# Attention and max-out feed-forward on one core: early columns first, casts shared, w's first half for both token spans, some loads later

## The chip, the core and the metric

One core of a Trainium2 chip runs the whole program. The metric is device time in microseconds (us); a run's *span*, from the first to the last instruction in the trace, is about 1.8 us shorter than its time. The kernel before takes 282.14 us (median of 3 runs, 282.08 to 282.3). Beside the experiments it ran again on four chips, from 282.14 to 286.01 in all, so every experiment is compared with runs of the kernel before from its own rounds, on the same chip. In the views PE is TensorE (it multiplies matrices), DVE is VectorE, ACT is ScalarE (here the exps and some copies), POOL is GpSimd and SP is SyncE (here it issues loads). PSUM is the memory that TensorE writes, SBUF the one that it reads.

## The reference, cut to what matters

```python
# q, k, v: (8 batches, 8 heads, 576 tokens, 64), float32
scores = q @ k.T / 8, masked so that 64-token block i sees blocks j <= i
x = (softmax(scores) @ v)               # -> (4608 tokens, 512)
g = maximum(x @ w1, x @ w2)             # (4608, 1024)
out = g @ w_out                         # (4608, 512)
```

## The kernel before: the parts that matter here

Heads are handled in pairs, two pairs to a group; a batch has 4 pairs (groups 0 and 1). A group's q and k are loaded, cast to bf16 (16-bit floats), transposed on TensorE, and copied from PSUM to SBUF. Scores of a pair come in bursts (p: the first 256 query tokens; q1, q2, q3: the rest), each followed by one exp on ACT. `av` multiplies by v and normalises, `x_out` transposes the result into x. Feed-forward matmuls (h: 8 *steps* for one 128-column slice f of w1 and w2) are poured in between by `fill`, in the order of a list of units; a unit waits until its tokens of x exist.

```python
def cast(nm, g, parts):                       # parts: (engine's copy, first, last row group)
    ...
def load_qk(g, queues, gated=False):          # gated: a small GpSimd memset of the target makes
    ...                                       # the DMA wait until GpSimd gets to this point
# order of issue in the opening
load_qk(1, (SP, SP)); load_qk(2, (SP, None))
...
load_v(0, 0); load_v(0, 1); load_w(0, 256, (0,))
cast("k", 1, ((pool, 0, RPP),))
load_w(0, 256, (1,)); load_qk(2, (None, SP), gated=True)
...
# TensorE order of the opening, cut
warm_up(16)                                   # 16 matmuls of zeros, "fillers"
...
burst_p(0); masks_p(0); burst_p(1); warm_up(2); masks_p(1)
load_v(0, 2); load_v(0, 3); load_v(0, 4); load_w(256, 256)
burst_q1(0); load_w(512, 512); warm_up(3)
burst_p(2); av(0, [0, 1]); burst_q3(0); warm_up(2); burst_p(3); ...
cast("q", 2, ((pool, 0, RPP),)); masks_q(0); cast("k", 2, ((pool, 0, RPP),))
burst_q2(1); x_out(1, 0, 2); ...              # the first h may start after this x_out
for c in range(3): load_v(1, c)
fill(2); load_qk(3, (SP, SP), gated=True)
...
masks_q(3); ...; fill(3)
tile_0(4), tile_1(4); av(3, [2, 3, 4]); fill(5); x_out(1, 2, NCH)   # end of batch 0's attention
# units: for each token span i, all 8 slices f
for i in range(NSPAN):
    for f in range(NFF):
        h(i, f)
```

GpSimd (POOL) is not only a caster: it issues the loads of v and w, writes the masks, and its memsets open the gates of the later q, k loads, all in program order.

The softmax here doesn't subtract the row's maximum and nothing guards it: scores larger than these inputs give would overflow.

Of the kernel before, what the change touches and what calls it, by code (L numbers as in the profile page):

```python
# [9 lines left out]
BF16 = mybir.dt.bfloat16  # L10
# [4 lines left out]
def kernel(  # L15
# [10 lines left out]
    nc = tc.nc  # L26

    B, H, S, D = q.shape
    P = 128
# [6 lines left out]
    NFF = d_ff // P  # L36
# [6 lines left out]
    NP = 64  # L43
    RPP = S // NP
# [9 lines left out]
    NCH = 5  # L54
# [3 lines left out]
    QCUT = 256  # L58
# [14 lines left out]
    NSPAN = len(spans)  # L73
# [37 lines left out]
    def load_qk(g, queues, gated=False):  # L111
        b, u = divmod(g, GPB)
        for nm, src, queue in (("q", q, queues[0]), ("k", k, queues[1])):
            if queue is None:
                continue
            raws[nm, g] = t = raw.tile([P, 2, RPP * D], FP32, name=f"{nm}raw")
            if gated:
                nc.gpsimd.memset(t[:, 0, :1], 0.0)
            queue.dma_start(
                out=t[:],  # L120
                in_=src[b, 4 * u:4 * u + 4].rearrange(
                    "(s h) (p t) d -> (h p) s (t d)", h=2, t=RPP),
            )

    def cast(nm, g, parts):
        t = raws.pop((nm, g)).rearrange("p s (t d) -> p t s d", d=D)
        qk_n[nm, g] = n = qkn.tile([P, RPP, 2, D], BF16, name=f"{nm}n")
        for copy, j0, j1 in parts:
            copy(out=n[:, j0:j1], in_=t[:, j0:j1])  # L129

# [11 lines left out]
    def load_w(f0, fw, which=(0, 1)):  # L142
        for i in which:
            dst, src = ((w1_sb, w1r), (w2_sb, w2r))[i]
            nc.gpsimd.dma_start(out=dst[:, :, f0:f0 + fw], in_=src[:, :, f0:f0 + fw])
# [11 lines left out]
    nc.vector.memset(zeros[:], 0.0)  # L157
    nc.scalar.activation(out=warm[:], in_=warm[:], func=AF.Exp)
    load_qk(1, (SP, SP))
    load_qk(2, (SP, None))  # L160
    make_identity(nc, ident)
    for r in range(NV):
        nc.vector.memset(vv_r[r][:, :, :, D:D + 1], 1.0)
# [7 lines left out]
    for c in range(2):  # L171
        load_v(0, c)
    load_w(0, 256, (0,))
    cast("k", 1, ((pool, 0, RPP),))
    load_w(0, 256, (1,))
    load_qk(2, (None, SP), gated=True)


    done_tokens = [0]
# [64 lines left out]
    def plan():  # L244
        def h(i, f):
            t0, w = spans[i]
            units.append((h_unit(i, f), t0 + w, w / SPAN, 2 * NDM))

        def y(i, s, last=False):
            t0, w = spans[i]  # L250
            if last:
                units.append((y_last(i, s), t0 + w, 0.333, 3 * NFF))
            else:
                units.append((y_unit(i, s), t0 + w, 1.0, NFF))

        for i in range(NSPAN):
            for f in range(NFF):
                h(i, f)
                if i > 2 and f % 2 == 0 and f // 2 < tiles[i - 1]:
                    y(i - 1, f // 2)  # L260
            if i == 1:
                for j in range(2):
                    for s in range(tiles[j]):
                        y(j, s)
        n = tiles[-1]
        for s in range(n):
            y(NSPAN - 1, s, s == n - 1)
# [13 lines left out]
    def fill(n):  # L281
        while n > 0 and at[0] < len(steps) and steps[at[0]][1] <= done_tokens[0]:
            u, _, cost = steps[at[0]]
            next(u)
            n -= cost
            at[0] += 1


    def warm_up(n):
        pw = ps_m.tile([P, SPAN], FP32, name="ps_w", tag="m")  # L290
        for _ in range(n):
            nc.tensor.matmul(pw[:], zeros[:, :P], zeros[:], start=True, stop=True)  # L292
# [4 lines left out]
    def transposes(nm, g, copies):  # L297
        n = qk_n.pop((nm, g))
        pts = [ps_m.tile([P, RPP, NP], BF16, name=f"ps_{nm}T", tag="m") for _ in range(2)]
        for j in range(RPP):  # L300
            for i in range(2):
                r = slice(i * NP, (i + 1) * NP)
                nc.tensor.transpose(  # L303
                    pts[i][:, j, :], n[r, j].rearrange("p s d -> p (s d)"), ident[r, r],
                )

        def copy_out(which=(0, 1)):
            for i in which:
                t = (qT_r if nm == "q" else kT_r)[(2 * g + i) % NT]
                copies[i](  # L310
                    out=t[:, :S].rearrange("q (p j) -> q p j", j=RPP),
                    in_=pts[i].rearrange("q j p -> q p j"),
                )
        return copy_out

# [44 lines left out]
    def burst_p(p):  # L360
        burst(p, ((0, 0, QCUT), (1, P, QCUT - P)), 0)

    def burst_q1(p):
        burst(p, ((0, QCUT, 320), (1, QCUT, 192)), 384)

    def burst_q2(p):
        burst(p, ((1, 448, P), (2, QCUT, 320), (4, 512, BLK)), 896)
# [4 lines left out]
    def masks_p(p, eng=None):  # L372
        for a in (0, 256):
            mask(p, a, eng)

    def masks_q(p, eng=None):
        for a in (1024, 1408):
            mask(p, a, eng)
# [34 lines left out]
    def av(p, ts):  # L413
        b, hp = divmod(p, HP)
        vv = vv_r[b % NV]
        a = aT_r[p % NA]
        n = len(ts)
        h0 = hp // 2 * 4 + hp % 2
        if p % 2 == 0 and ts[0] == 0:
            xps[p // 2] = xpool.tile([P, NCH, 2, 2, D], BF16, name="xp")  # L420
        xp = xps[p // 2]
        po = ps_m.tile([P, n, 2, D + 1], FP32, name="ps_o", tag="m")
        n_mm = 2 * sum(t + 1 for t in ts)
        mm = 0
        for gi, t in enumerate(ts):
            for hh in range(2):
                for c in range(t + 1):
                    a0 = a_col(p, c, t)
                    nc.tensor.matmul(  # L429
                        po[:, gi, hh, :], a[:, hh, a0:a0 + P], vv[:, c, h0 + 2 * hh, :],  # L430
                        start=(mm == 0), stop=(mm == n_mm - 1),
                    )
                    mm += 1
        rec = small.tile([P, 3, 2, 1], FP32, name="rec")
        nc.vector.reciprocal(rec[:, :n, :, 0], po[:, :, :, D])  # L435
        nc.vector.tensor_mul(  # L436
            xp[:, ts[0]:ts[0] + n, :, p % 2], po[:, :, :, :D],
            rec[:, :n].to_broadcast([P, n, 2, D]),
        )

    def x_out(g, t0=0, t1=NCH):
        b, u = divmod(g, GPB)
        xp = xps[g]
        n = t1 - t0
        n_odd = min(t1, NCH - 1) - t0
        pe = ps_m.tile([P, 2, n, BLK], BF16, name="ps_xe", tag="m")
        po = ps_m.tile([P, 2, n_odd, BLK], BF16, name="ps_xo", tag="m")
        for s in range(2):
            for t in range(t0, t1):
                src = xp[:, t, s].rearrange("p a d -> p (a d)")  # L450
                nc.tensor.transpose(pe[:, s, t - t0, :], src[:BLK], ident[:BLK, :BLK])  # L451
                if t < NCH - 1:
                    nc.tensor.transpose(po[:, s, t - t0, :], src[BLK:], ident[BLK:, BLK:])
        dst = xT[:, 2 * u:2 * u + 2, b * S + t0 * P:b * S + t1 * P].rearrange(
            "p s (t h w) -> p s t h w", h=2, w=BLK)
        nc.vector.tensor_copy(out=dst[:, :, :, 0], in_=pe[:])  # L456
        nc.vector.tensor_copy(out=dst[:, :, :n_odd, 1], in_=po[:])
        if u == GPB - 1:
            done_tokens[0] = min(b * S + t1 * P, (b + 1) * S)

# [37 lines left out]
        return lambda: [f() for f in outs]  # L498


    warm_up(16)
    cq = transposes("q", 0, (dve, act))
    ck = transposes("k", 0, (act, dve))
    cq((0,))
    ck((0,))
    cq((1,))
    ck((1,))
    cast("q", 1, ((dve, 0, RPP),))
    burst_p(0)
    masks_p(0)  # L510
    burst_p(1)
    warm_up(2)
    masks_p(1)
    for c in range(2, NCH):
        load_v(0, c)
    load_w(256, 256)
    cq = transposes("q", 1, (dve, dve))
    burst_q1(0)
    ck = transposes("k", 1, (dve, dve))
    for i in range(2):  # L520
        cq((i,))
        ck((i,))
    load_w(512, 512)
    warm_up(3)
    burst_p(2)
    av(0, [0, 1])
    burst_q3(0)
    warm_up(2)
    burst_p(3)
    masks_p(2, nc.vector)  # L530
    av(1, [0, 1])
    masks_p(3, nc.vector)
    burst_q2(0)
    av(2, [0, 1])
    warm_up(2)
    burst_q1(1)
    av(3, [0, 1])
    x_out(0, 0, 2)
    warm_up(2)
    cast("q", 2, ((pool, 0, RPP),))  # L540
    masks_q(0)
    cast("k", 2, ((pool, 0, RPP),))
    burst_q2(1)
    x_out(1, 0, 2)
    warm_up(2)
    burst_q3(1)
    masks_q(1)
    for c in range(3):
        load_v(1, c)
    fill(2)  # L550
    load_qk(3, (SP, SP), gated=True)
    burst_q1(2)
    transposes("q", 2, (dve, act))()
    fill(3)
    burst_q2(2)
    av(0, [2, 3, 4])
# [5 lines left out]
    av(1, [2, 3, 4])  # L562
    fill(2)
    burst_q1(3)
    transposes("k", 2, (dve, act))()
    pad_keys(4)
    pad_keys(5)
    fill(2)
    x_out(0, 2, NCH)
    burst_q2(3)  # L570
    av(2, [2, 3, 4])
    fill(2)
    burst_q3(3)
# [87 lines left out]
```

## Time and profile before

| | before |
|---|---|
| time, span | 282.14 us, 280.4 us |
| TensorE busy, share of the chain that ended last | 96%, 91% |
| mean granted TensorE clock | 1.000 |
| fillers | 29 |
| first h, steps done before the last x_out of batch 0 | 18.09 us, 40 |
| q, k of group 2: cast by GpSimd at | 17.20, 18.81 us |

The prediction below shows the chain and TensorE's opening (start, duration, engine, line, operation, tiles; in brackets the idle time before it and what ended that). Here is the row of events that turned out to decide the case, GpSimd in order of time (start, duration, engine, line, operation, tiles; in brackets the idle time before it and what ended that):

```profile
17.20 1.14 POOL L129 CAST qn<-qraw 128x1152 bf16<-128x1152 f32 x1
...
18.81 1.15 POOL L129 CAST kn<-kraw 128x1152 bf16<-128x1152 f32 x1
...
20.30 2.64 POOL L133 DMA_DIRECT2D vv<-in_v_dram  x3
...
22.99 0.10 POOL L118 MEMSET qraw<- 128x1 f32 x1
...
23.19 0.34 POOL L350 MEMSET aT<- 64x128 bf16 x2
...
26.06 0.20 POOL L350 MEMSET aT<- 64x128 bf16 x1 [0.45 <-ACT aT L345]
...
29.60 1.15 POOL L129 CAST qn<-qraw 128x1152 bf16<-128x1152 f32 x1 [2.44 <-DMA qraw<-in_q_dram]
```

Group 2 is cast early, without waiting for its data. So the next three v issues, the gate of group 3 (22.99) and the masks of pair 2 (23.19) are all on time; those of pair 3 (from 26.06) waited for the exp and not for GpSimd. The 2.44 us of waiting at 29.60 show up in no TensorE wait: nothing urgent stands behind that cast.

### The profile page before, as it was taken

The numbers are of one execution on the slowest core, as the hardware profiler recorded it, in microseconds if no ns is written. First come the engines' busy times: TensorE is split into PE (matmuls) and PEld (weight loads), VectorE is DVE, ScalarE is ACT, GpSimd is POOL, SyncE is SP. The second block draws the span as 40 slices with busy tenths as digits, with TensorE's granted clock in tenths as the row PEclk, the third lists the DMA queues.
The fourth block names the chain that finished last, engine by engine and source line by source line (L and its number), as shares of the span: only waits on it lengthen the run. The fifth ranks groups of instructions, "written<-read, shape, count | busy, mean of one in ns | idle before, by whom it ended". The sixth has DMA issues, their size and how long they took to land.

```text
span 280.4 us, 7767 instructions
## 1 busy us (share of the span) xinstructions
PE 269.3 (96%) x3208; PEld 151.5 (54%) x3253; DVE 185.7 (66%) x386; ACT 139.6 (50%) x194; POOL 107.7 (38%) x271
## 2 busy tenths in 40 slices
PE   7699999999999999999999999999999999999995
PEld 2356766655556455555555554646455644444543
DVE  5967879668887676767667576757655766365430
ACT  3786577667664664655647374664653000100112
POOL 2996446764654625164344625371120000000000
PEclk9999999999999999999999999999999999999999
DMA  7999999979934994479266866175301111111114
GB/s 261 263 219 220 187 244 273 250 148 189 210 42 153 154 156 78 178 82 239 49 208 77 219 75 196 52 81 50 67 5 49 49 54 40 39 75 40 73 41 150
DMA packets 55940, 36.68 MB, mean 131 GB/s; under 512 B 38752, under 2 KB 43232, under 8 KB 55904
## 3 DMA queue, kind: packets, MB, share of 16 engines
q0 software_dynamic: 41728, 7.87, 35.0%
q1 hardware_dynamic: 13760, 27.66, 28.8%
q10 hardware_dynamic: 416, 0.66, 0.7%
q8 instruction: 25, 0.41, 0.6%
q14 instruction: 11, 0.09, 0.1%
HBM read 34.60 MB, written 9.44 MB: 157 GB/s over the span
## 4 chain that ended last, share of the span: by engine, by line
PE 91%; DMA 4%; issue 2%; ACT 1%; DVE 1%; POOL 0%; ACTq 0%
PE ps_h L197 43%; PE ps_y L215 22%; PE ps_o L429 11%; PE ps_s L321 8%; DMA vv<-in_v_dram 2%; PE ps_xe L451 2%; PE ps_qT L303 2%; DMA qraw<-in_q_dram 2%; PE ps_kT L303 2%; ACT aT L345 1%; PE ps_s L339 1%; PE ps_y L231 1%; PE ps_w L292 1%; DVE g L206 0%; POOL vv L133 0%
## 5 line engine op out<-in xcount | busy, mean ns | idle before, releaser
L197 PE MATMUL ps_h<-xT,w_sb 128*128 128x512 bf16 (+3 forms) x605 | 136.2, 357 | 1.7 <-issue 0.3
L345 ACT ACTIVATE aT<-ps_s 128x1024 bf16<-128x1024 f32 (+2 forms) x100 | 96.2, 996 | 17.2 <-PE ps_s L321 16.2
L197 PEld LDWEIGHTS <-w_sb 128*128 128x128 bf16 x640 | 57.8, 98 | 57.4 <-issue 8.1
L204 DVE CAST h<-ps_h 128x512 bf16<-128x512 f32 (+3 forms) x80 | 50.9, 637 | 28.9 <-PE ps_h L197 26.7
L215 PE MATMUL ps_y<-wo_sb,g 128*128 128x512 bf16 x273 | 65.5, 379 | 2.1 <-PE ps_s L321 1.3
L206 DVE TENSOR_TENSOR g<-h,ps_h 128x512 bf16<-128x512 bf16 (+3 forms) x80 | 50.6, 632 | 12.0 <-PE ps_h L197 10.5
L350 POOL MEMSET aT<- 64x128 bf16 x124 | 22.3, 199 | 92.7 <-ACT aT L345 91.3
L221 ACT COPY y<-ps_y 128x512 f32<-128x512 f32 x31 | 18.1, 584 | 70.3 <-PE ps_y L215 56.5
L429 PEld LDWEIGHTS <-aT 128*128 128x128 bf16 x960 | 37.3, 98 | 14.1 <-issue 1.3
L215 PEld LDWEIGHTS <-g 128*128 128x128 bf16 x280 | 26.8, 98 | 30.4 <-issue 1.1
L429 PE MATMUL ps_o<-vv,aT 128*128 128x65 bf16 x960 | 39.9, 194 | 0.3 <-DMA vv<-in_v_dram 0.3
L133 POOL DMA_DIRECT2D vv<-in_v_dram x40 | 33.7, 847 | 0.5
L436 DVE TENSOR_TENSOR xp<-ps_o,rec 128x256 bf16<-128x256 f32 (+1 forms) x64 | 31.4, 491 | 2.2
L321 PE MATMUL ps_s<-qT,kT 64*128 64x64 bf16 (+6 forms) x344 | 31.6, 279 | 1.1 <-ACT kT L310 0.7
L435 DVE RECIPROCAL rec<-ps_o 128x4 f32<-128x4 f32 (+1 forms) x64 | 12.0, 188 | 20.6 <-PE ps_o L429 18.9
L310 ACT COPY qT<-ps_qT 128x576 bf16<-128x576 bf16 x15 | 9.6, 638 | 29.4 <-PE ps_qT L303 29.4
L187 POOL COPY g<-g 128x512 bf16<-128x512 bf16 x8 | 4.9, 611 | 38.3 <-DVE g L206 38.2
L129 POOL CAST kn<-kraw 128x1152 bf16<-128x1152 f32 x15 | 17.3, 1151 | 5.2 <-DMA kraw<-in_k_dram 5.1
L129 POOL CAST qn<-qraw 128x1152 bf16<-128x1152 f32 (+1 forms) x15 | 16.5, 1099 | 7.0 <-DMA qraw<-in_q_dram 6.9
L456 DVE COPY xT<-ps_xe 128x640 bf16<-128x640 bf16 (+2 forms) x18 | 8.2, 453 | 15.7 <-PE ps_xe L451 14.9
L310 ACT COPY kT<-ps_kT 128x576 bf16<-128x576 bf16 x15 | 9.6, 638 | 15.0 <-PE ps_kT L303 15.0
L321 PEld LDWEIGHTS <-kT 64*128 64x128 bf16 x344 | 13.2, 95 | 6.6 <-issue 2.8
(44 smaller groups left out, 144.5 us busy)
## 6 DMA issues: line engine op xcount, KB each, us to landing
qraw<-in_q_dram SPq DMA_DIRECT2D x16, 576.0 KB, 4.1
out_dram<-y SPq DMA_DIRECT2D x35, 256.0 KB, 2.1
kraw<-in_k_dram SPq DMA_DIRECT2D x15, 576.0 KB, 5.4
vv<-in_v_dram POOLq DMA_DIRECT2D x32, 128.0 KB, 5.3
w_sb<-in_moe_w_dram POOLq DMA_DIRECT2D x4, 256.0 KB, 6.6
w_sb<-in_moe_w_dram POOLq DMA_DIRECT2D x2, 512.0 KB, 10.7
wo_sb<-in_moe_w_out_dram POOLq DMA_DIRECT2D x2, 512.0 KB, 11.8
kraw<-in_k_dram ACTq DMA_DIRECT2D x1, 576.0 KB, 5.4
```

Of the source, the lines that this page charges most:

```text
L129: copy(out=n[:, j0:j1], in_=t[:, j0:j1])
L133: nc.gpsimd.dma_start(out=vv_r[b % NV][P - rows:, c, :, :D], in_=v[b, :, c * P:c * P + rows, :].rearrange("h p d -> p h d"),)
L197: nc.tensor.matmul(pt[:, :w], w_sb[:, c, f * P:(f + 1) * P], xT[:, c, t0:t0 + w], start=(c == 0), stop=(c == NDM - 1),)
L204: nc.vector.tensor_copy(out=h1[:, :w], in_=pt[:, :w])
L206: nc.vector.tensor_max(g[:, f, m:m + w], h1[:, :w], pt[:, :w])
L215: nc.tensor.matmul(py[:], g[:, f, s * P:(s + 1) * P], wo_sb[:, f, :], start=(f == 0), stop=(f == NFF - 1),)
L310: copies[i](out=t[:, :S].rearrange("q (p j) -> q p j", j=RPP), in_=pts[i].rearrange("q j p -> q p j"),)
L321: nc.tensor.matmul(ps[:, hh, col:col + w], kT[r, k0:k0 + P], qT[r, q0:q0 + w], start=True, stop=True,)
L345: nc.scalar.activation(out=aT_r[p % NA][:, :, a0:a0 + w], in_=ps[:, :, :w], func=AF.Exp, scale=scale,)
L350: (eng or nc.gpsimd).memset(aT_r[p % NA][BLK:, :, a0:a0 + BLK], 0.0)
L429: nc.tensor.matmul(po[:, gi, hh, :], a[:, hh, a0:a0 + P], vv[:, c, h0 + 2 * hh, :], start=(mm == 0), stop=(mm == n_mm - 1),)
L436: nc.vector.tensor_mul(xp[:, ts[0]:ts[0] + n, :, p % 2], po[:, :, :, :D], rec[:, :n].to_broadcast([P, n, 2, D]),)
```

## The change

The intent: get to the first scores sooner by copying only the columns that they need, share group 1's casts between two engines, replace fillers by real h steps, and avoid needing w's second half early. To make room for w, the loads were reordered too: v's last chunks go behind w's second quarter, and q, k of group 2 are loaded late, behind a gate. The diff, cut to its core:

```diff
     load_qk(1, (SP, SP))
-    load_qk(2, (SP, None))
@@
-    cast("k", 1, ((pool, 0, RPP),))
+    cast("q", 1, ((pool, 6, RPP),))
+    cast("k", 1, ((pool, 4, RPP),))
     load_w(0, 256, (1,))
-    load_qk(2, (None, SP), gated=True)
@@ units
-        for i in range(NSPAN):
-            for f in range(NFF):
+        for f0 in (0, NFF // 2):
+            for i in range(2):
+                for f in range(f0, f0 + NFF // 2):
+                    h(i, f)
+        for i in range(1, NSPAN):
+            for f in range(NFF if i > 1 else 0):
@@ the opening (LOW: columns 0 to 260 of qT, kT; HIGH: the other 315)
-    cq((0,)) ; ck((0,)) ; cq((1,)) ; ck((1,)) ; cast("q", 1, ((dve, 0, RPP),))
+    cq((0,), LOW) ; ck((0,), LOW) ; ck((1,), LOW) ; cq((1,), LOW) ; cq((0,), HIGH)
+    cast("q", 1, ((dve, 0, 6),)) ; cast("k", 1, ((dve, 0, 4),))
     burst_p(0) ; masks_p(0)
+    cq((1,), HIGH) ; ck((0,), HIGH)
     burst_p(1)
+    ck((1,), HIGH)
     ...
+    load_w(256, 256)
     for c in range(2, NCH): load_v(0, c)
-    load_w(256, 256)
+    load_qk(2, (SP, SP), gated=True)
+    load_w(512, 512)
     ... group 1's copies in halves, those of k's second half and x's first copies on ACT ...
     ... q bursts of pairs 0 and 1: six before the first h become two; 29 fillers become 24 ...
+    burst_q3(1) ; masks_q(1)
+    cast("q", 2, ((pool, 0, RPP),)) ; cast("k", 2, ((pool, 0, RPP),))
     for c in range(3): load_v(1, c)
```

More of the change, by code (lines that the diff above doesn't have):

```diff
@@ L125, in cast @@
     def cast(nm, g, parts):
-        t = raws.pop((nm, g)).rearrange("p s (t d) -> p t s d", d=D)
-        qk_n[nm, g] = n = qkn.tile([P, RPP, 2, D], BF16, name=f"{nm}n")
+        t = raws[nm, g].rearrange("p s (t d) -> p t s d", d=D)
+        if (nm, g) not in qk_n:
+            qk_n[nm, g] = qkn.tile([P, RPP, 2, D], BF16, name=f"{nm}n")
+        n = qk_n[nm, g]
         for copy, j0, j1 in parts:
@@ L305, in transposes, with copy_out @@
                 )
-        def copy_out(which=(0, 1)):
+        def copy_out(which=(0, 1), part=(0, NP), copy=None):
+            p0, p1 = part
             for i in which:
                 t = (qT_r if nm == "q" else kT_r)[(2 * g + i) % NT]
-                copies[i](
-                    out=t[:, :S].rearrange("q (p j) -> q p j", j=RPP),
-                    in_=pts[i].rearrange("q j p -> q p j"),
+                (copy or copies[i])(
+                    out=t[:, p0 * RPP:p1 * RPP].rearrange("q (p j) -> q p j", j=RPP),
+                    in_=pts[i][:, :, p0:p1].rearrange("q j p -> q p j"),
                 )
@@ L439, in av, with x_out @@
         )
-    def x_out(g, t0=0, t1=NCH):
+    def x_out(g, t0=0, t1=NCH, copies=(dve, dve)):
         b, u = divmod(g, GPB)
@@ L455, in x_out @@
             "p s (t h w) -> p s t h w", h=2, w=BLK)
-        nc.vector.tensor_copy(out=dst[:, :, :, 0], in_=pe[:])
-        nc.vector.tensor_copy(out=dst[:, :, :n_odd, 1], in_=po[:])
+        copies[0](out=dst[:, :, :, 0], in_=pe[:])
+        copies[1](out=dst[:, :, :n_odd, 1], in_=po[:])
         if u == GPB - 1:
@@ L498, in t_pair @@
         return lambda: [f() for f in outs]
+    LOW = (0, -(-QCUT // RPP))
+    HIGH = (LOW[1], NP)
     warm_up(16)
@@ L503 @@
     ck = transposes("k", 0, (act, dve))
-    cq((0,))
-    ck((0,))
-    cq((1,))
-    ck((1,))
-    cast("q", 1, ((dve, 0, RPP),))
+    cq((0,), LOW)
+    ck((0,), LOW)
+    ck((1,), LOW)
+    cq((1,), LOW)
+    cq((0,), HIGH)
+    cast("q", 1, ((dve, 0, 6),))
+    cast("k", 1, ((dve, 0, 4),))
     burst_p(0)
     masks_p(0)
+    cq((1,), HIGH)
+    ck((0,), HIGH)
     burst_p(1)
+    ck((1,), HIGH)
     warm_up(2)
     masks_p(1)
+    load_w(256, 256)
     for c in range(2, NCH):
         load_v(0, c)
-    load_w(256, 256)
-    cq = transposes("q", 1, (dve, dve))
-    burst_q1(0)
-    ck = transposes("k", 1, (dve, dve))
-    for i in range(2):
-        cq((i,))
-        ck((i,))
-    load_w(512, 512)
-    warm_up(3)
-    burst_p(2)
-    av(0, [0, 1])
-    burst_q3(0)
-    warm_up(2)
-    burst_p(3)
-    masks_p(2, nc.vector)
-    av(1, [0, 1])
-    masks_p(3, nc.vector)
-    burst_q2(0)
-    av(2, [0, 1])
-    warm_up(2)
-    burst_q1(1)
-    av(3, [0, 1])
-    x_out(0, 0, 2)
-    warm_up(2)
-    cast("q", 2, ((pool, 0, RPP),))
-    masks_q(0)
-    cast("k", 2, ((pool, 0, RPP),))
+    load_qk(2, (SP, SP), gated=True)
+    load_w(512, 512)
+    cq = transposes("q", 1, (dve, act))
+    ck = transposes("k", 1, (dve, dve))
+    cq((0,), LOW)
+    cq((1,), LOW)
+    ck((0,), LOW)
+    ck((1,), LOW)
+    cq((0,), HIGH, act)
+    cq((1,), HIGH, dve)
+    warm_up(2)
+    burst_p(2)
+    ck((0,), HIGH, act)
+    av(0, [0, 1])
+    masks_p(2, nc.vector)
+    burst_p(3)
+    av(1, [0, 1])
+    ck((1,), HIGH, act)
+    masks_p(3, nc.vector)
+    warm_up(1)
+    av(2, [0, 1])
+    x_out(0, 0, 2, (act, act))
+    warm_up(1)
+    av(3, [0, 1])
+    burst_q1(0)
+    warm_up(1)
+    x_out(1, 0, 2, (dve, dve))
+    burst_q2(0)
+    warm_up(1)
+    fill(2)
+    burst_q3(0)
+    masks_q(0)
+    burst_q1(1)
+    fill(1)
     burst_q2(1)
-    x_out(1, 0, 2)
-    warm_up(2)
+    fill(1)
     burst_q3(1)
     masks_q(1)
+    cast("q", 2, ((pool, 0, RPP),))
+    cast("k", 2, ((pool, 0, RPP),))
     for c in range(3):
@@ L552 @@
     burst_q1(2)
-    transposes("q", 2, (dve, act))()
     fill(3)
@@ L564 @@
     burst_q1(3)
+    transposes("q", 2, (dve, act))()
+    fill(2)
+    x_out(0, 2, NCH)
+    burst_q2(3)
     transposes("k", 2, (dve, act))()
@@ L567 @@
     pad_keys(5)
-    fill(2)
-    x_out(0, 2, NCH)
-    burst_q2(3)
     av(2, [2, 3, 4])
```

## The prediction

> **What bounds the kernel now.** I read the shares of the engines first, then the chain that ended last, then the instructions in order of time over the first 50 us, because every edit lies there.
>
> ```profile
> PE 269.3 (96%) x3208; PEld 151.5 (54%) x3253; DVE 185.7 (66%) x386; ACT 139.6 (50%) x194; POOL 107.7 (38%) x271
> PE 91%; DMA 4%; issue 2%; ACT 1%; DVE 1%; POOL 0%; ACTq 0%
> ```
>
> TensorE is busy 96% of 280.4 us and carries 91% of the chain. Useful TensorE work is the same in both kernels, so the time is that work plus what TensorE spends waiting or on filler matmuls of zeros. Both kinds of waste lie in the opening: in the window from 8 to 18 us there are 13 filler matmuls; after 18 us TensorE is busy 11.83 of the next 12 us.
>
> ```profile
> 1.24 5.23 PE L292 MATMUL ps_w<-zeros 128*128 128x512 bf16 x16 [1.24 <-DVE zeros L157]
> 8.44 0.34 PE L321 MATMUL ps_s<-qT,kT 64*128 64x256 bf16 x4 [0.73 <-ACT kT L310]
> 10.12 0.44 PE L303 MATMUL ps_qT<-ident,qn 64*128 64x64 bf16 x18 [0.47 <-DVE qn L129]
> 12.14 0.34 PE L321 MATMUL ps_s<-qT,kT 64*128 64x256 bf16 x4
> 18.09 0.61 PE L197 MATMUL ps_h<-xT,w_sb 128*128 128x256 bf16 x4
> 27.60 0.92 PE L429 MATMUL ps_o<-vv,aT 128*128 128x65 bf16 x24
> 28.35 1.25 PE L197 MATMUL ps_h<-xT,w_sb 128*128 128x256 bf16 x10
> 30.06 1.99 PE L197 MATMUL ps_h<-xT,w_sb 128*128 128x256 bf16 x16
> ```
>
> Columns are start, duration, engine, line. Scores begin at 8.44 after a copy by ACT, transposes of group 1 at 10.12 after a DVE cast, scores of pair 2 at 12.14, the first real feed-forward matmul (h) at 18.09. The last two lines matter most: the ten h steps at 28.35 fill the time in which DVE normalises the last attention output of batch 0, and the sixteen at 30.06 run while DVE copies its transposes.
>
> ```profile
> 10.59 0.76 DVE L310 COPY qT<-ps_qT 128x576 bf16<-128x576 bf16 x1 [0.53 <-PE ps_qT L303]
> 26.41 0.49 ACT L345 ACTIVATE aT<-ps_s 128x384 bf16<-128x384 f32 x1 [0.47 <-PE ps_s L321]
> 28.79 0.56 DVE L436 TENSOR_TENSOR xp<-ps_o,rec 128x384 bf16<-128x384 f32 x1
> 30.45 0.35 DVE L456 COPY xT<-ps_xe 128x384 bf16<-128x384 bf16 x1
> ```
>
> **What the Trainium skill says.** "ScalarE: Activation LUTs", section "What ACT_TABLE_LOAD costs": 186 ns plus 0.833 ns per element, with about 93 ns of overlap back to back. The trace agrees: 1024 columns took 1.02 us (1.04 by the rule), a 576-column copy 0.64 (0.67). Half copies of 261 and 315 columns are then estimated at 0.38 and 0.43 us. "VectorE: DVE Perf Modes", section on the TRN2 errata: from PSUM (120+N)/0.96 ns; 576 columns give 0.725 us and the trace has 0.756, so the halves are about 0.42 and 0.47. "TensorE: Matmul & The Clock Gate", Part 1: the array starts at half clock until about 3.4 us of activity. The first 16 fillers took 5.23 us, 327 ns each, against about 216 warm; no idle gap I foresee reaches 3.4 us. "DMA: Bandwidth & Descriptors", section "Issuing engines are not separate DMA queues": all queues share 16 engines. The trace fits: v loads land after 5.6 us early and after 11.4 to 13 us when w and q, k loads are in flight.
>
> **The change part by part.** All times below are my in-order reckoning from durations of the rows above.
>
> *Early columns first.* The first scores need 256 of 576 columns. ACT's half copy of k ends near 8.1 instead of 8.39, so scores start near 8.15 (0.3 us sooner). But ACT now runs two high halves between the first two exps (0.81 us each, 128x768), so the second exp ends near 10.9 instead of about 10.35.
>
> *Shared casts.* DVE's 1.34 us cast of q in group 1 becomes 6/9 of q and 4/9 of k, about 0.9 + 0.6 us; GpSimd takes the rest, about 0.5 + 0.7. The q transposes move to about 9.85 (from 10.12), those of k to about 10.5 (from 10.61): DVE serialises casts and half copies, so little is won.
>
> *Group 1's copies to ACT.* The next filler pair needs a PSUM buffer that frees only when ACT's high half follows the second exp, at about 11.55. Scores of pair 2 then start near 12.05 against 12.14, their exp ends near 13.2 instead of 13.33, and pair 3's exp at 14.35 instead of 15.12, since the long exp of the first q burst (1.02) and that of the third (0.49) now come later. The two token tiles of x follow sooner: first h near 17.0 instead of 18.09, 1.1 us gained. But before, six wide score bursts of pairs 0 and 1 were done by then; now two are. The four missing ones cost TensorE 0.19+0.33+0.33+0.19 = 1.04 us. Net of the opening: about 0. Five fillers fewer (24 instead of 29) are what made room.
>
> *ACT in the middle.* ACT gains four half copies (about 1.6 us) and two x copies (about 0.7) that DVE had, and starts the q-burst exps at about 15.4 where before three of them, those of pair 0, were already done by 16.1. From there it owes 4 x (1.02+1.02+0.49) = 10.1 us of exps and 1.3 us of copies. Even packed, that ends at 26.8, and with gaps of about 1.4 us at 28.2, against 26.90 before. TensorE waits for its two score buffers: about +0.7 us.
>
> *The order of w.* Only the first half of w is now used on the first 256 tokens: 4 x 8 = 32 matmul steps. The fills before the second token span is ready sum to 2+1+1+2+3+1+2+2+2 = 16 units of two steps: exactly the 32. The next unit needs tokens up to 576, which are ready only after the last x_out, so the fills of 3 and 5 that follow do nothing. Before, 40 steps were done by then and 24 stood in reserve. TensorE now goes straight to the last burst's exp (0.49 plus about 0.4 of signalling and mask, partly under 0.54 of scores: 0.4 idle), then waits for DVE's reciprocal and multiply (28.45 to 29.54 before: 1.1 idle) and for the x copies (0.6 idle). Sum 2.1 us, of which before shows some 0.2: +1.9 us. The skipped steps are done later at their usual cost. What the order buys, not waiting for w's second half, is worth nothing against this trace: I find no TensorE wait for w there, though the last half-w load landed at 28.3, just before its first use near 29.
>
> *Loads.* q, k of group 2 (2 x 576 KB) are issued near 15.3 instead of 2.26 and 11.13, and their casts (2 x 1.15 us on GpSimd) come after the masks of pair 1, near 21.5, instead of 17.2. GpSimd then still owes five v issues (0.85 each) before the last masks. Those masks may be late by 0 to 1 us: +0.4.
>
> Sum: 0 + 0.7 + 1.9 + 0.4 = +3.0 us, that is 285.1.
>
> **The rivals.** *The fillers are the gain.* Five fewer at 0.215 us is 1.08 us off TensorE's queue; if the voids close because something else runs there (the later, fuller ACT leaves ready scores, and a fill is at hand sooner), the time is 281.1. For it: the fills sum to exactly the 32 available steps, which looks like deliberate tuning, and early DMA is relieved of 576 KB. Against it: in program order nothing stands between the last normalisation and its transposes. *GpSimd or late q, k become the bound.* If k of group 2 lands near 24 instead of 17.4, its cast holds back the v issues and the masks of pairs 2 and 3, each up to 1 us: 286 to 287. For it: GpSimd was busy 9.51 of the 10 us from 8 to 18, and k of group 3 made it wait 2.07 us. *Nothing moves the end.* The voids might be repaid later, where h of 256 columns is held by DVE (16 steps in 1.99 us from 30.06 against 10 in 1.25): then about 282.
>
> **Range and chances.** A hand-made list of five engines tends to add waits that overlap in truth, so I weigh my sum twice and the filler rival once: (2 x 285.1 + 281.1) / 3 = 283.8. Each uncertain term is about 1 us, so eight times in ten 280.9 to 286.2. Faster by 2% means under 276.5, more than all filler and idle time between 8 and 18 us could give back: 0.01. Slower by 2% means over 287.8, the GpSimd rival on top of my sum: 0.05. Within: 0.94.
>
> **What would show it.** Right: first h near 17, scores of pair 2 still near 12, TensorE idle about 1 us before the last x_out of batch 0 and about 0.6 after it, with 32 h steps before it; h resumes near 32 instead of 30.06. Wrong: h steps within those waits, exps of the q bursts ending by 27, or TensorE waiting for casts of group 2 or for v. If the first h comes before 16, the opening is better than my lists and the total goes under 282.

## The result, and the profile after

| | before | after |
|---|---|---|
| median, range, runs | 282.15 us, 282.08 to 282.3, 4 | 291.87 us, 290.66 to 293.69, 4 |
| ratio, 95% interval | | 1.0349, 1.0294 to 1.0404 |
| span, mean clock of the profiled run | 280.4, 1.000 | 289.9, 0.982 |

A ratio here is the mean time of one kernel's runs over that of the other's runs of the same rounds, so it is not quite the ratio of the medians quoted. Executions over 1.5% slower than the fastest of the same kernel are left out of the means. The change is 3.5% slower, outside the predicted 280.9 to 286.2 and in the class that I gave 5%.

TensorE after, in order of time; these lines answer to the prediction's:

```profile
17.52 0.60 PE L198 MATMUL ps_h<-xT,w_sb 128*128 128x256 bf16 x4
...
24.66 0.86 PE L436 MATMUL ps_o<-vv,aT 128*128 128x65 bf16 x15 [1.78 <-DMA vv<-in_v_dram]
...
32.04 0.84 PE L436 MATMUL ps_o<-vv,aT 128*128 128x65 bf16 x22 [2.26 <-POOL aT L357]
...
37.02 0.23 PE L458 MATMUL ps_xe<-ident,xp 64*128 64x64 bf16 x1 [0.88 <-DVE xp L443]
...
37.45 3.64 PE L198 MATMUL ps_h<-xT,w_sb 128*128 128x320 bf16 x15
...
41.85 2.21 PE L198 MATMUL ps_h<-xT,w_sb 128*128 128x320 bf16 x15
```

The first h comes at 17.52, near the forecast 17.0. Then TensorE waits for v, for a mask, and for the normalisation. It resumes h at 37.45 with 32 steps done, where before it resumed at 30.06 with 40. That is 7.39 us, plus 8 steps at about 0.11 us (ten took 1.09 in the chain of before), together 8.3 us. The next 15 steps take 3.64 us against 2.21 for the same number four microseconds later, another 1.4. The sum, 9.7 us, is the whole difference between the medians. (The 7.39 us hold some half clock too: the 24 attention matmuls at 34.63 took 1.50 us against 0.92 before.) Nothing is lost or won later: the transposes of k of group 4, and of group 15, the last, start 9.7 and 9.5 us later than before. Two lines of before, then two of after:

```profile
45.03 0.44 PE L303 MATMUL ps_kT<-ident,kn 64*128 64x64 bf16 x18
...
195.77 0.44 PE L303 MATMUL ps_kT<-ident,kn 64*128 64x64 bf16 x18
...
54.71 0.44 PE L309 MATMUL ps_kT<-ident,kn 64*128 64x64 bf16 x18
...
205.24 0.44 PE L309 MATMUL ps_kT<-ident,kn 64*128 64x64 bf16 x18
```

GpSimd after, in the same columns as above:

```profile
24.80 1.14 POOL L131 CAST qn<-qraw 128x1152 bf16<-128x1152 f32 x1 [3.19 <-DMA qraw<-in_q_dram]
27.86 1.15 POOL L131 CAST kn<-kraw 128x1152 bf16<-128x1152 f32 x1 [1.92 <-PE ps_qT L309]
28.95 2.63 POOL L135 DMA_DIRECT2D vv<-in_v_dram  x3
31.55 0.14 POOL L118 MEMSET qraw<- 128x1 f32 x1
...
31.78 0.34 POOL L357 MEMSET aT<- 64x128 bf16 x2
...
38.82 1.15 POOL L131 CAST qn<-qraw 128x1152 bf16<-128x1152 f32 x1 [4.21 <-DMA qraw<-in_q_dram]
```

The casts of group 2 now wait for their data, 7.6 and 9.1 us later than before. (The profile puts the second wait down to a transpose. That k was issued at 16.13 and took 11.6 us to land, at about 27.7, just before the cast. In run 12 below it landed at about 25.3 and was cast at 25.43, ahead of those transposes at 26.01, so it is the DMA that the cast waits for.) Everything behind them on GpSimd is late too: the gate of group 3 by 8.6 us, the masks of pair 2 by 8.6 us (31.78; TensorE waits for them until 32.04), and group 3's own cast by 9.2 us. Issues of q and k of group 2 after (size, us from issue to landing):

```profile
qraw<-in_q_dram SPq DMA_DIRECT2D x1, 576.0 KB, 8.9
kraw<-in_k_dram SPq DMA_DIRECT2D x1, 576.0 KB, 11.6
```

The clock, from the stretches of the changed kernel (busy us of PE, PEld, DVE, ACT, POOL with counts; then granted clock, DMA share, GB/s):

```profile
11.00:12.00 1.00, 0.62 (x19) 0.51 (x19) 0.83 (x3) 0.59 (x2) 0.97 (x5) 1.00 1.27 164
...
13.00:14.00 1.00, 1.00 (x11) 0.59 (x12) 0.86 (x5) 1.00 (x3) 1.00 (x3) 0.50 1.02 124
...
30.00:32.00 2.00, 0.00 (x0) 0.00 (x0) 0.39 (x1) 0.78 (x2) 1.94 (x6) 1.00 1.07 69
...
35.00:36.00 1.00, 1.00 (x21) 0.96 (x18) 0.00 (x0) 0.96 (x2) 0.00 (x0) 0.50 1.05 331
```

TensorE is at half clock twice, from about 12.9 to 16.3 us and from about 33.4 to 40.2 us, each time after a thin or idle stretch.

**Theories.** *Loads*: the late q, k of group 2 and the late v make the waits, and the clock only follows. *w order*: the starved fills are the main loss. *Clock*: the half clock is a cost of its own. *Opening*: the new order of TensorE costs by itself.

### The profile page after: what moved, and what is told of

Read it like the earlier page. It is cut to its first block, busy times and chain, and to the rows that moved or that the text cites. A ratio compares the mean times of both kernels' runs of the same rounds, so it can differ in the third digit from the quotient of the medians.

```text
span 289.9 us, 7810 instructions
## 1 busy us (share of the span) xinstructions
PE 277.9 (96%) x3248; PEld 153.7 (53%) x3248; DVE 184.9 (64%) x387; ACT 141.8 (49%) x202; POOL 108.2 (37%) x273
## 4 chain that ended last, share of the span: by engine, by line
PE 88%; DMA 5%; POOL 4%; DVE 1%; issue 0%; ACT 0%
PE ps_h L198 44%; PE ps_y L216 21%; PE ps_o L436 10%; PE ps_s L328 7%; DMA vv<-in_v_dram 4%; POOL vv L135 2%; PE ps_qT L309 2%; DMA qraw<-in_q_dram 2%; PE ps_xe L458 2%; PE ps_kT L309 2%; POOL w_sb L147 1%; POOL kn L131 1%; PE ps_y L232 1%; PE ps_s L346 1%; POOL qn L131 0%
## 5 line engine op out<-in xcount | busy, mean ns | idle before, releaser
L198 PE MATMUL ps_h<-xT,w_sb 128*128 128x512 bf16 (+3 forms) x640 | 143.0, 361 | 0.1
L216 PE MATMUL ps_y<-wo_sb,g 128*128 128x512 bf16 x280 | 66.5, 379 | 0.0
L436 PEld LDWEIGHTS <-aT 128*128 128x128 bf16 x960 | 38.5, 99 | 18.7 <-issue 3.6
L436 PE MATMUL ps_o<-vv,aT 128*128 128x65 bf16 x960 | 41.3, 196 | 4.2 <-POOL aT L357 2.3
L317 ACT COPY qT<-ps_qT 128x576 bf16<-128x576 bf16 (+2 forms) x18 | 10.6, 587 | 32.5 <-PE ps_qT L309 32.3
L131 POOL CAST qn<-qraw 128x1152 bf16<-128x1152 f32 (+2 forms) x16 | 17.4, 1085 | 11.9 <-DMA qraw<-in_q_dram 11.9
L131 POOL CAST kn<-kraw 128x1152 bf16<-128x1152 f32 (+1 forms) x15 | 16.9, 1124 | 5.5 <-PE ps_qT L309 4.1
L317 ACT COPY kT<-ps_kT 128x576 bf16<-128x576 bf16 (+2 forms) x18 | 10.6, 590 | 15.5 <-PE ps_kT L309 15.4
```

Of the source, the lines that this page charges most:

```text
L131: copy(out=n[:, j0:j1], in_=t[:, j0:j1])
L198: nc.tensor.matmul(pt[:, :w], w_sb[:, c, f * P:(f + 1) * P], xT[:, c, t0:t0 + w], start=(c == 0), stop=(c == NDM - 1),)
L216: nc.tensor.matmul(py[:], g[:, f, s * P:(s + 1) * P], wo_sb[:, f, :], start=(f == 0), stop=(f == NFF - 1),)
L317: (copy or copies[i])(out=t[:, p0 * RPP:p1 * RPP].rearrange("q (p j) -> q p j", j=RPP), in_=pts[i][:, :, p0:p1].rearrange("q j p -> q p j"),)
L436: nc.tensor.matmul(po[:, gi, hh, :], a[:, hh, a0:a0 + P], vv[:, c, h0 + 2 * hh, :], start=(mm == 0), stop=(mm == n_mm - 1),)
```

## The experiments

Each was timed in 3 rounds (one in 5) beside the kernel before. One per cent is 2.8 us. All results are correct.

**1. Loads back.** The changed kernel with the loads in the old order:

```diff
+    load_qk(2, (SP, None))                         # after load_qk(1, ...)
+    load_qk(2, (None, SP), gated=True)             # after load_w(0, 256, (1,))
-    load_w(256, 256); v chunks 2-4; load_qk(2, (SP, SP), gated=True); load_w(512, 512)
+    v chunks 2-4; load_w(256, 256); load_w(512, 512)
```

> The changed kernel with the loads in the order of before (q, k of group 2 early; v ahead of w's second quarter); opening and w order stay changed. Loads theory: the 1.8 us wait for v, the 2.3 us wait for the masks and the half clock that follows them all come from the late loads, so the time falls by 5 to 7 us to 285 to 287, near the 285.1 that the prediction's sum gave without them. Rival, w order (the starved fills with the clock drop are the main loss): the waits go but TensorE still idles at the end of batch 0 and the half clock stays, time 288 or more.

Measured: 285.63 us (284.89 to 286.16), ratio 1.0098 (1.0071 to 1.0125), clock 0.994 to 1.0. The loads account for 3.49 - 0.98 = 2.5%, about 7 us of the 9.7. Both long waits are gone from its trace.

**2. w order back**, loads still late:

```diff
-        for f0 in (0, NFF // 2): ...
+        for i in range(NSPAN):
+            for f in range(NFF):
```

> The changed kernel with the w order of before; late loads stay. Loads theory: the waits for v and for the masks stay, only the last 1.5 us of idle is filled with h steps, time 288.5 to 290.5. W-order rival: the starved stretch was the main loss and its fills also keep the clock up, time under 287.

Measured: 289.86 us, ratio 1.0252 (1.0227 to 1.0278). On top of the late loads the new order of w costs about 1%; the mask wait of 2.2 us stays. As the loads theory said.

**3. Opening alone** (1 and 2 together):

> Changed opening (early columns, split casts, TensorE order, fewer fillers) with loads and w order of before. Loads theory and the prediction's own sum: opening about 0 and ACT backlog at most +0.7, so 281.5 to 283. Rival that the opening itself costs (ACT backlog, GpSimd casts late): 284 or more.

Measured: 285.25 us (284.38 to 286.84), ratio 1.0106 (1.0068 to 1.0143). This is a miss: the opening alone loses about 3 us. The profiled run had full clock, three others 0.988 to 0.994.

**4. w order alone on the kernel before:**

```diff
-        for i in range(NSPAN): ...
+        for f0 in (0, NFF // 2): ...               # as in the change
```

> The kernel before with nothing changed but the order of w's halves. The prediction's +1.9 us for starvation: 283.5 to 284.5, full clock, TensorE idle about 1 us before the last x_out of batch 0. Rival that the order is worth nothing or something (steps only deferred): 281.5 to 282.5.

Measured: 283.04 us (282.97 to 283.31), ratio 1.0010 (0.9990 to 1.0030). My +1.9 us is refuted; the median lies between the two expected bands. Its TensorE waits in the first 60 us:

```profile
PE ps_xe L455 <- DVE xp L440: 0.7, 1, 0.7
...
PE ps_h L197 <- DVE xT L461: 0.3, 1, 0.3
```

The two idle stretches are there, 1.0 us in all. But h resumes at 29.79 us against 30.06, since the empty fills no longer stand in the way: the net loss there is 8 steps, 0.9 us, less the 0.27. The traces do not show it repaid: the transposes of k of group 15 start at 196.59 against 195.77, 0.8 us later. That is one trace of each kernel; the interval of the runs allows -0.3 to +0.8 us.

**5. Fillers in the late idle stretches:**

```diff
+    warm_up(10)                                    # before av(2, [2, 3, 4])
+            warm_up(4)                             # before x_out(1, 2, NCH)
```

> The changed kernel with 10 filler matmuls put where TensorE waits 2.3 us for the masks and 4 where it waits for the last normalisation of batch 0; they take about 3 us of time that was idle. Clock theory: the half clock from 34 to 40.5 us follows those idle stretches and costs by itself about 2.3 us (15 h steps in 3.64 us instead of 2.1, 24 attention matmuls in 1.50 instead of 0.9), so 288.5 to 290 with a mean clock of 0.99 or more. Rival, the clock is incidental: 291 to 293, more if the fillers are in the way.

Measured: 291.85 us, ratio 1.0293 (1.0222 to 1.0365), in the rival's band. Not a clean test: in its trace k of group 2 came later still, TensorE cooled before the fillers, and they ran at half clock.

```profile
32.37 2.87 PE L298 MATMUL ps_w<-zeros 128*128 128x512 bf16 x8 [0.22 <-issue]
```

**6. v first**, the only edit being the order of v's chunks 2 to 4 and w's second quarter:

```diff
-    load_w(256, 256)
     for c in range(2, NCH): load_v(0, c)
+    load_w(256, 256)
```

> The changed kernel with v's last three chunks issued ahead of w's second quarter, nothing else. If waits add up: the 1.8 us wait for v goes and the time falls to about 289.5. If late k of group 2 sets the masks anyway (its cast runs at 27.9 us, the masks at 31.8), TensorE only waits longer for the masks: 291 to 292, mask wait 3 us or more.

Measured: 291.06 us (288.98 to 292.01), ratio 1.0238 (1.0147 to 1.0328), not told apart from the change by these runs. In the trace the v wait is gone, but TensorE waits 2.4 us for the masks and 0.8 for the cast of k (2.3 and none in the change): about half of what v gave back is waited for elsewhere.

**7. q, k of group 2 early**, v still behind w:

```diff
+    load_qk(2, (SP, None))
+    load_qk(2, (None, SP), gated=True)
-    load_qk(2, (SP, SP), gated=True)
```

> The changed kernel with q, k of group 2 loaded as before; w's second quarter stays ahead of v. Late-q,k theory: the mask wait goes, the clock stays up, 286.5 to 288.5; the v wait of about 1 to 2 us stays. v-order rival: v is the main loss, so 290 or more.

Measured: 285.66 us (285.16 to 286.55), ratio 1.0075 (1.0006 to 1.0145). This one edit does as much as restoring all loads. A v wait of 1.1 us remains in its trace and costs nothing that can be seen in the total.

**8. Masks on VectorE:**

```diff
-    masks_q(2)                    ->    +    masks_q(2, nc.vector)
-    masks_q(3)                    ->    +    masks_q(3, nc.vector)
```

> The changed kernel with the last two pairs of masks of batch 0 on VectorE instead of GpSimd, loads unchanged. GpSimd theory: the 2.3 us wait is only that the masks queue behind the late cast and v issues, so it goes and the clock drop with it: 287 to 289.5. Rival, the late k itself is the bound (its transposes and what follows): 290 to 292.

Measured: 290.67 us (289.44 to 293.66), ratio 1.0264 (1.0173 to 1.0355). Inconclusive, though the median lies in the rival's band. The mask wait vanishes, but in the profiled run TensorE waits 3.6 us for v instead, with half clock after it, and the gate of group 3 is still at 31.41 us.

**9. More fillers, ahead of every wait** (26: 8 before the first late attention outputs, 8 before and 6 after the transposes of k of group 2, 4 before the last x_out):

```diff
+    warm_up(8)    # before av(0, [2, 3, 4])
+    warm_up(8)    # before transposes("k", 2), and +warm_up(6) after
+            warm_up(4)    # before x_out(1, 2, NCH)
```

> The changed kernel with 26 filler matmuls at the four places where TensorE stood idle, put ahead of each wait: 8 before the first late attention outputs, 8 before and 6 after the transposes of k of group 2, 4 before the last x_out. The kernel with fillers only late was no clean test: its fillers ran at half clock. Clock theory: clock 0.998 or more and 288 to 290. Rival (what is waited for sets the time, the clock only eats into idle): 291 to 292.5 in spite of a full clock.

Measured: 291.63 us (289.96 to 292.38), ratio 1.0298 (1.0236 to 1.0359), clock 0.999 or more in three of four runs. The clock is repaired and the time is not. The profiled run, at clock 0.999, resumes h at 37.56 us, and then waits for group 3 where the changed kernel was crawling:

```profile
40.81 0.44 PE L309 MATMUL ps_qT<-ident,qn 64*128 64x64 bf16 x18 [0.61 <-POOL qn L131]
...
44.35 0.44 PE L309 MATMUL ps_kT<-ident,kn 64*128 64x64 bf16 x18 [0.50 <-POOL kraw L118]
```

In this trace the half clock mostly ate into time that the late data would have taken anyway: these two waits sum to 1.1 us, and the half clock had cost the 15 steps 1.4. What the 26 fillers cost by themselves was not measured.

**10. Opening alone with five fillers back:**

```diff
-    warm_up(2)  ->  +    warm_up(3)     # after the first two bursts
-    warm_up(1)  ->  +    warm_up(2)     # at four places before the first h
```

> The opening alone with five fillers back, 29 in all as before. If the opening's 2.4 us is the clock drop of some of its runs (0.988 to 0.994 in three of four): clock 0.999 or more in all runs and 283.5 to 284.5. If it is ACT's backlog and the later score bursts: 285 to 286, since each filler takes 0.2 us where TensorE waits anyway or pays for it.

Measured: 284.47 us (284.0 to 285.25), ratio 1.0055 (0.9995 to 1.0114), full clock in three of four runs. It lies at the edge of the clock theory's band, and its interval overlaps that of run 3: by the means the missing fillers are about half of the opening's loss, which is not shown. The runs at full clock (0.999 or more) say the same: in runs 3, 10 and 15 they took 284.38, 284.0 to 284.61, and 283.99 and 285.04 us, 1.3 to 2.3 us above the median of before in their rounds. So some 1.3 us or more of the opening's 3 us is there without a low clock.

**11. Early columns and shared casts only**, on the kernel before (the cast and copy lines of the diff, nothing else):

```diff
+    cq((0,), LOW) ... ck((1,), HIGH)               # group 0 as in the change
+    cast("q", 1, ((dve, 0, 6),)) ; cast("k", 1, ((dve, 0, 4),)) ; the rest on GpSimd
```

> The kernel before with only the early columns of group 0 and the shared casts of group 1; TensorE order, fillers, copies of group 1, loads and w order of before. If early columns and casts are harmless and the opening loses by moving score bursts behind the first x tiles and copies to ACT: 281.5 to 283. If the high halves between the two exps and the serialised casts on VectorE cost by themselves: 284 or more.

Measured: 284.09 us (282.15 to 284.23), ratio 1.0023 (0.9967 to 1.0080): the same as before within noise. The profiled run, 284.11 us, had one wait that would explain its distance from 282.15 (the other runs have no trace):

```profile
31.25 0.61 PE L200 MATMUL ps_h<-xT,w_sb 128*128 128x256 bf16 x4 [1.82 <-DMA w_sb<-in_moe_w_dram]
```

**12. w's second half later**, after the last masks of batch 0:

```diff
-    load_w(512, 512)              # after load_qk(2, ...)
+    load_w(512, 512)              # after masks_q(3)
```

> The changed kernel with w's second half issued some 13 us later, after the last masks of batch 0; q, k of group 2 still late. If the 8.9 and 11.6 us of landing come from sharing the 16 DMA engines with w's second half: q, k land 5 to 7 us after issue, the mask wait falls under 0.7 us, time 286 to 288. If late issue alone is at fault: 290 to 292.

Measured: 292.66 us, ratio 1.0304 (1.0220 to 1.0388); one of its runs (295.46) was slow and is left out of the ratio. q and k landed after 8.1 and 9.1 us instead of 8.9 and 11.6, and the mask wait fell to 1.2 us, so sharing the DMA engines with w is part of k's delay. But TensorE then waited 2.9 us for w's second half itself, so the total tells nothing.

**13. GpSimd's order mended**, loads as late as in the change:

```diff
     masks_q(1)
-    cast("q", 2, ...) ; cast("k", 2, ...)
     for c in range(3): load_v(1, c)
     load_qk(3, (SP, SP), gated=True)
+    cast("q", 2, ((pool, 0, RPP),))
     ...
     masks_q(2)
+    cast("k", 2, ((pool, 0, RPP),))
```

> The changed kernel with only GpSimd's order mended: v issues of batch 1, the gate of group 3's loads and the masks of pair 2 stand ahead of the casts that wait for late data. In-order theory: the 2.3 us mask wait goes, group 3 is loaded some 7 us sooner, 286 to 288.5; the v wait stays. Landing theory (late k of group 2 by itself delays transposes and all after): 289.5 to 292.

Measured: 287.92 us (287.36 to 288.6), ratio 1.0184 (1.0161 to 1.0208). GpSimd in its trace:

```profile
25.53 0.10 POOL L118 MEMSET qraw<- 128x1 f32 x1
...
26.81 0.20 POOL L357 MEMSET aT<- 64x128 bf16 x1
...
28.41 1.14 POOL L131 CAST kn<-kraw 128x1152 bf16<-128x1152 f32 x1 [0.85 <-PE ps_s L328]
...
32.76 1.15 POOL L131 CAST qn<-qraw 128x1152 bf16<-128x1152 f32 x1
```

The cast of k is as late as in the change (28.41 against 27.86), yet the masks come at 26.81, group 3's gate opens 6.0 us sooner and its q is cast 6.1 us sooner. Merely letting nothing urgent stand behind the late casts returns 1.65%, 4.7 us of the loads' 7. The in-order theory holds. In the trace TensorE no longer waits for the masks (2.26 us in the change) and the half clock after that wait is gone; the wait for v stays, 1.6 us.

**14. Group 0 and the order of w together**, on the kernel before (11 and 4), in 5 rounds:

> The kernel before with early columns of group 0, shared casts and the new order of w; loads, TensorE order and fillers of before. Theory: no waits for w's second half, so 281.8 to 283 in all runs, same as before or up to 0.3% faster. Rival, the starved fills cost what was predicted (+1.9): 284 or more.

Measured: 283.32 us (282.93 to 283.54), ratio 1.0019 (1.0004 to 1.0033). No wait for w in its trace, and no run beyond 283.54. The median misses the expected band by 0.3 us; it is no faster than before. Against run 11's wait of 1.82 us this is what the order of w is for, seen in one trace of each.

**15. Opening alone, copies as before:** group 1's copies whole and on VectorE, x copies on VectorE, TensorE's order as changed:

```diff
-    cq = transposes("q", 1, (dve, act)) ; halves, four of them on ACT
+    cq = transposes("q", 1, (dve, dve)) ; whole copies
-    x_out(0, 0, 2, (act, act))
+    x_out(0, 0, 2)
```

> The opening alone, but with group 1's copies whole and on VectorE and the x copies on VectorE as before; score bursts and fillers stay in the changed order. ACT theory: relieved of about 2.3 us of copies, ACT runs the late score bursts sooner, 282.5 to 284. Order theory: the bursts come behind the x tiles whoever copies, 284.5 to 286.

Measured: 285.09 us (283.99 to 285.16), ratio 1.0076 (1.0055 to 1.0096). Taking the copies off ACT does not repair the opening: against run 3 it is 0.3% less, and the two intervals overlap. Its ACT in order of time:

```profile
14.33 0.81 ACT L350 ACTIVATE aT<-ps_s 128x768 bf16<-128x768 f32 x1 [0.63 <-PE ps_s L326]
17.52 6.96 ACT L350 ACTIVATE aT<-ps_s 128x1024 bf16<-128x1024 f32 x8 [2.39 <-PE ps_s L326]
```

ACT is idle for 2.39 us because no scores come, then owes eight exps without a gap. Before, the first q burst's exp already ran at 10.81 us, in a hole.

No version that was run beats the kernel before. The nearest, w's order alone, is level with it.

## Why the prediction was wrong, step by step

**The step that failed is the one on the loads**: "Those masks may be late by 0 to 1 us: +0.4". Measured, the loads' order costs 2.5 to 2.7% (runs 1 and 7), about 7 us. The delay was thought to end at the last masks, at 0 to 1 us. TensorE waited 2.26 us for masks, and 1.78 us for v, for which the sum has no term although the prediction's own list has it as a sign of being wrong. I placed the two casts of group 2 near 21.5 us; they ran at 24.80 and 27.86. I had seen what the step needed: v landing after 11.4 to 13 us when w, q and k are in flight, and the full GpSimd. In the sum I then put no landing time on q and k at all. Issue at 15.72 and 16.13 plus 8.9 and 11.6 us gives the casts. With 6.3 us, the landing of k before, q and k would have landed near 22 and the step would still have looked small. My GpSimd rival named this mechanism with k near 24 and stopped at the masks: 286 to 287. It left out that the gate of group 3's loads stands in the same queue, so that the delay is handed on (31.55 against 22.99). Run 13 shows that what stands behind the casts in the queue is most of the loss, not the late landing alone. How it splits between masks and gate is not shown: run 8 took the masks alone out of the queue and settled nothing, and in the changed kernel's own trace TensorE does not wait for group 3, where in run 9's it does (0.61 and 0.50 us).

**The starved fills** (+1.9): mechanism seen, size wrong. The two waits that I named near 1.1 and 0.6 us measure 0.7 and 0.3 in run 4, and the total moved by 0.1% (-0.1 to +0.3%), 0.8 us in the traces. The empty fills shorten the way to the last x_out by 0.27 us; my third rival ("the voids might be repaid later") is not borne out, since that lag stays to the end. On top of the changed opening the order cost nothing that can be seen (run 1 against run 3), but under late loads about 1%, 2.7 us (the change against run 2).

**The opening** (0 in the opening, +0.7 in ACT's middle): first h near 17 was right (17.52; 17.18 in run 3), scores of pair 2 near 12 too (12.34). The sum was too small: 1.06% (0.68 to 1.43%) measured. Shared casts and early columns show no cost beyond noise (runs 11 and 14). By elimination, what costs is TensorE's new order with fewer fillers: four score bursts moved behind the first x tiles, and ACT first idles and then has a backlog (the trace of run 15). No run puts back the order alone. ACT's extra copies, which I blamed, are not most of it (run 15). Part of it may be a cooler clock from fewer fillers, up to about half (run 10).

**The clock.** I wrote that no idle gap reaches 3.4 us and left it at that. No gap before either half-clock stretch of the changed kernel was that long, and the clock fell all the same. It accounts for about 2 us in that trace (1.4 in the 15 steps, 0.6 in the 24 attention matmuls), but in run 9 the time at full clock is not told apart from 291.87, so it is not shown to be an addend.

**The weighting** of the filler rival (281.1) had no run in its favour; 285.1 alone would have been in the range's upper part and still far too low. What the change gave, earlier first h and fewer fillers, was real and small, and was lost to new waits. (The 13 fillers from 8 to 18 us are those of the program; the trace has records of 10.)

## What to carry to other kernels

When a load is moved later, write down its landing under the traffic of that moment, then list everything that stands behind its consumer on the same in-order engine: issues, masks and gates of later loads are delayed with it, and the delay is handed on to the next group. Place work that waits for data behind work that others wait for, as run 13 did. When early real work takes the place of fillers, look at what it pushes back: here it was the score bursts that feed ACT, and the opening lost 1%.

## What the Trainium skill lacked or had wrong

- "TensorE: Matmul & The Clock Gate", Part 1, gives one idle window of about 3.4 us for the return to half clock. Here a stretch without any matmul record of about 2.3 us (29.8 to 32.04) came before the half clock from about 33.4 us, and the one from about 12.9 us followed no gap over 0.7 us, only thin work: TensorE busy 0.94 us of the two from 10 to 12. (Of many short idles the page tells only for another kernel, without a figure.) The two half-clock stretches lasted about 3.4 and 6.8 us, which agrees with the page's window. The page's half rate at the start agrees too, although the views read 1.00 there: the first 16 fillers took from 5.18 us to 6.59 us in the traces, where three took 0.81 us later (before, at 11.40).
- The same page's specification table has GpSimd as a strict first-in first-out queue. Run 13 agrees and shows the price in this kernel, which no page has: 4.7 us from two casts placed ahead of v issues, masks and a load gate.
- "DMA: Bandwidth & Descriptors", on issuing engines, says that all queues share the engines. That section has no figure for what that does to a load in flight: the same 576 KB took 5.0 us with few others, 8.9 and 11.6 us beside v and w, and 8.1 and 9.1 us without w's second half.
